# Re-planned RWKV and MLP-mixer kernel: new transfer costs, wide transposes of u, a row of w by matmul, and zero products in the head

## The chip, the cores and the metric

The kernel runs on one core of one Trainium2 chip. The metric is the device time of one execution in microseconds (us). A core has five engines with instruction streams of their own: TensorE (PE; its weight loads are listed as PEld), VectorE (DVE), ScalarE (ACT), GpSimd (POOL) and SyncE (SP), and 16 DMA engines that move data for all of them. Each stream runs in order; streams wait for one another through semaphores.

## The reference

A linear-attention recurrence with per-channel decay (RWKV) gives `x`, and a token-and-channel MLP mixer follows. B = 4 batches, H = 8 heads, S = 768 steps, D = 48 channels per head; `x` is 768 x 384 per batch.

```python
def _attn_ref(r, k, v, w, u):
    state = np.zeros((B, H, D, D))
    for t in range(S):
        kt, vt, rt = (k[:, :, t], v[:, :, t], r[:, :, t])
        cur = np.einsum('bhd,bhe->bhde', u[None] * kt, vt)
        y[:, :, t] = np.einsum('bhd,bhde->bhe', rt, state + cur)
        state = w[None, :, :, None] * state + np.einsum('bhd,bhe->bhde', kt, vt)
    return y

def _moe_ref(x, w_tok1, w_tok2, w_ch1, w_ch2):
    xt = x.transpose(0, 2, 1)
    h = np.maximum(xt @ w_tok1, 0.0) @ w_tok2       # 768 -> 256 -> 768, over tokens
    u = x + h.transpose(0, 2, 1)
    h2 = np.maximum(u @ w_ch1, 0.0) @ w_ch2         # 384 -> 1536 -> 384, over channels
    return u + h2
```

Note that the name `u` stands for two things: the bonus row `u` of the recurrence (8 x 48 numbers, an input beside the decay row `w`), and the mixer's middle value `u` (768 x 384 per batch, `u_sb` in the kernel, `uT` when turned).

## The kernel before, in words

**Tiling.** The recurrence is done in chunks of T = 128 steps: 24 *units*, six per batch (C = 6), numbered over all batches. Powers of the decay are folded into `k` and `r` with two tables per position in a group of G = 3 chunks: `wn` (for `k`) and `wp` (for `r`), made on ACT from `lnw = ln w`. For one unit:

- `load` brings k, r and v (192 KB each; tiles `ld_k`, `ld_r`, `ld_v`), issued by SP.
- `kp` and `rp` multiply k and r by their tables into `kpr` (POOL or DVE, as the plan chooses); `vb` casts v on ACT.
- k and r are turned: either on TensorE (`tr`, eight 128x128 transposes into PSUM, copied out by `rk` on ACT) or by one DMA transpose that SP issues (`turn_unit`). `CFG["turned"]` lists the units that use DMA.
- `at` is the 128x128 product of the turned k and r for every head, in two PSUM tiles of four heads; `AT` masks each into SBUF on DVE. In units of `CFG["raw"]` the second tile is first cast by ACT (`raw`) and then masked from SBUF (`ATr`).
- `pr`, `pg`, `adg` and `yd` give the bonus term, `kv` and `S` the state, `yS` and `y` the output of the chunk, and `x` adds `y` and `yd` into the batch's `x_b`.

**The mixer of a batch.** `hid` accumulates the token product into two PSUM tiles while units finish; `hr` is its relu; for each of the six chunks `bk` is the way back and `us` adds it to `x_b` (tile `u_sb`). Then `u` is turned: in batches of `pe_turn` on TensorE (`tu`, three transposes per chunk, copied out by `uT`), in the others by one DMA transpose per chunk (`uTd`). Each half of a batch (`sg`, three chunks) then has 12 `z` steps (three products each, relu by `zr`) and, for each chunk, 12 products `h`, with `os` and the store `out` behind them. The four weight matrices are fetched by POOL's DMA queue.

**The order.** No loop sets the order of the work. `graph` describes all steps with their engine, busy time and the time until a reader sees the result; `Plan.run` is a list scheduler over these numbers, which picks for every step an engine and a start. The kernel emits the steps in order of planned start, and each engine's order is kept as emitted. The plan's times are never used on the chip: only the order and the choice of engine come from them. Loads are held back by buffer space (eight units ahead); the loads of unit 6 also wait for `rp` of unit 5, so that the weights pass first. Tiles in PSUM beyond those of the recurrence share four buffers (pool `psM`, tag "m"); the plan keeps count of them in `banks`.

**The start.** `w` is broadcast to 128 partitions by a DMA of 192 KB on ACT's queue (`w_bc`); `w` and `u` are also loaded as eight rows each (`rows`) by SP after the first v, for a small product `wu`. TensorE runs eight products on a tile of zeros (`idle`) before the first real one.

Of the kernel before, what the change touches and what calls it, by code (L numbers as in the profile page):

```python
# [20 lines left out]
Ln = ACTF.Ln  # L21

B, H, S, D = 4, 8, 768, 48
T = 128
# [20 lines left out]
class Plan:  # L45
# [3 lines left out]
    def __init__(self, banks, busy_until, in_flight):  # L49
        self.steps, self.banks, self.busy_until, self.in_flight = [], banks, busy_until, in_flight  # L50

# [19 lines left out]
    def run(self):  # L71
# [5 lines left out]
        while todo:  # L77
# [4 lines left out]
            while again:  # L82
                again = False
                for s in sorted(open_, key=lambda s: (s.rank, s.ready)):
                    if s.ready > now or (s.take and min(banks) > now):
                        continue
                    if s.sends is not None and len(sent) >= self.in_flight:
                        old = sent[-self.in_flight]
                        if old.seen is None or old.seen > now:
                            if old.seen is not None:  # L90
                                heapq.heappush(times, old.seen)
                            continue
                    way = min(s.ways, key=lambda w: max(now, free.get(w[0], 0.0)) + w[2] + (w[4] if len(w) > 4 else 0.0))
                    eng, busy, seen = way[:3]
                    shares = len(way) > 3 and way[3]
                    if free.get(eng, 0.0) > now:
                        continue
                    if shares and port["DVE" if eng == "POOL" else "POOL"] > now:
                        heapq.heappush(times, max(port.values()))
                        continue  # L100
                    s.engine, s.start, s.end, s.seen = eng, now, now + busy, now + seen
                    free[eng] = s.end
                    if s.sends is not None:
                        sent.append(s.sends)
                    if shares:
                        port[eng] = s.end
                    heapq.heappush(times, s.end)
                    if s.take:
                        i = banks.index(min(banks))
                        banks[i], held[s.name] = float("inf"), i  # L110
                    for g in s.give:
                        banks[held.pop(g)] = s.seen
                        heapq.heappush(times, s.seen)
# [10 lines left out]
        return sorted(self.steps, key=lambda s: s.start)  # L124


MM = 0.1625
# [6 lines left out]
def graph(do, cfg):  # L134

    p = Plan(4, cfg.get("busy_until", dict(ACT=3.0, DVE=3.3, POOL=3.6)), cfg.get("in_flight", 8))
    unit_rank = cfg.get("unit_rank", lambda u: u)
# [7 lines left out]

    tables = {0: p.add("tables0", [("ACT", 1.6, 1.75)], rank=-100, emit=do("tables", 0))}
    setup = tables[0]
    for g in (1, 2):
        tables[g] = p.add(f"tables{g}", [("ACT", 1.05, 1.2)], [setup], rank=g - 0.6, emit=do("tables", g))

    wu = p.add("wu", [("PE", 0.6, 0.8)], rank=0.05, emit=do("wu"))
    uw = p.add("uw", [("DVE", 0.65, 0.8)], [wu], rank=0.05, emit=do("uw"))
# [4 lines left out]
    for n, (kind, i) in enumerate(cfg["transfers"]):  # L157
        if kind == "u":
            for nm in cfg.get("lorder", "krv"):
                s = p.add(f"i:{nm}{i}", [("SP", 0.45, 0.6)], fetched[-1:], rank=-1000 + n, emit=do("load", nm, i))  # L160
                fetched.append(s)
                gates[nm, i] = s
                loads[nm, i] = p.transfer(f"x:{nm}{i}", s, 0.93, 1.9, 0.0)
        else:
# [3 lines left out]
    def weight(i, after):  # L168
        s = p.add(f"i:w{i}", [("POOL", 0.9, 1.0, True)], after, rank=-50, emit=do("weight", i))
        took = cfg.get("wtime", (3.3, 3.0, 7.0, 7.8))[i]  # L170
        wx[i] = p.transfer(f"x:w{i}", s, took, took + 1.0, -1.0)

    p.wait(wu, [loads["v", 0]])
    wafter = cfg["wafter"]
    xs, S_prev, at_free, y_free, kv_read, yS_prev = {}, None, [], None, None, None
    kv_first, bank_read = None, []
    for u in range(NU):
# [9 lines left out]
        kp = p.add(f"kp{u}", [POOL2, DK], [loads["k", u], tab, old], rank=r, emit=do("kp", u))  # L187
        rp = p.add(f"rp{u}", [POOL2, DK], [loads["r", u], tab, old], rank=r + 0.1, emit=do("rp", u))
        for i, after in wafter.items():
# [51 lines left out]
    for b in range(B):  # L241
# [8 lines left out]
        hr = [p.add(f"hr{b}_{i}", [ACT1, DVEP], [h], give=[f"hid{b}_bank{i}"], rank=r, emit=do("hr", b, i)) for i in range(2)]  # L250
        uT = []
        for c in range(C):
# [5 lines left out]
            else:  # L258
                s = p.add(f"i:uT{b}_{c}", [("SP", 1.25, 1.3)], [us], rank=-3000 + c, emit=do("uTd", b, c))
                uT.append(p.transfer(f"x:uT{b}_{c}", s, 0.4, 1.3, 0.0))  # L260
        for sg in range(2):
# [7 lines left out]
            for si in range(3):  # L269
# [4 lines left out]
                downs[-1].append(s)  # L274
                s = p.add(f"i:o{b}_{c}", [("SP", 0.35, 0.4)], [s], rank=-1500, emit=do("out", b, c))
                stores.append(p.transfer(f"x:o{b}_{c}", s, 0.6, 1.8, 0.0))
    rng = random.Random(cfg.get("seed", 0))
# [19 lines left out]
def kernel(  # L297
# [53 lines left out]
    act.preload_act_table_set("natural_log_exp_and_others")  # L351


    idle = const.tile([128, 512], bf16, name="idle")
    dve.memset(idle, 0.0)
    idle_ps = psM.tile([128, 512], f32, name="idle_ps", tag="m")
    for _ in range(CFG.get("warm", 0)):
        pe.matmul(idle_ps, idle[:, 0:128], idle, start=True, stop=True)


    rows = const.tile([2 * HP, 2, P], f32, name="rows")
    dve.memset(rows, 1.0)
    iota_i = const.tile([128, 2, G], i32, name="iota_i")
# [42 lines left out]

    def tables(eng, g):
        if g == 0:
            act.activation(lnw, w_bc, Ln)
        act.activation(wn[:, g, :], lnw, Exp, scale=iota[:, 1, g:g + 1])  # L410
        act.activation(wp[:, g, :], lnw, Exp, scale=iota[:, 0, g:g + 1])

# [5 lines left out]
    def uw(eng):  # L418
        dve.tensor_copy(wu_sb, M0["wu"])
        for q in range(2):  # L420
            half = slice(q * P, q * P + P)
            dve.tensor_mul(UW[half, :, q], wu_sb[half, 0, :], wu_sb[half, 1, :])

    wtok1 = wts.tile([128, 6, dtok], bf16, name="wtok1")
# [10 lines left out]
    def load(eng, nm, i):  # L435
# [8 lines left out]
        loaded[nm, i] = t  # L444
        if (nm, i) == ("v", 0):
            for j, src in enumerate((w, u)):
                sp.dma_start(rows[j * HP:j * HP + HP, :, 0:D], src.rearrange("(a q) d -> a q d", q=2))
            if wide:
                sp.dma_start(out=u_bc, in_=u.rearrange("h d -> (h d)")[None, :].to_broadcast([128, dm]))

# [145 lines left out]
    def hid(eng, b, c):  # L596
        if c == 0:
            M[b]["h1"] = [psM.tile([128, dm], f32, name="h1_ps", tag="m") for _ in range(2)]
            M[b]["h1r"] = mpool.tile([128, 2, dm], bf16, name="h1r")
            M[b]["u"] = mpool.tile([128, C, dm], bf16, name="u_sb")  # L600
            M[b]["uT"] = mpool.tile([128, 3, S], bf16, name="uT")
        for i in range(2):
# [24 lines left out]
    def uT(eng, b, c):  # L627
        to = M[b]["uT"][:, :, ts(c, 128)]
        if eng == "ACT":
# [3 lines left out]

    def uTd(eng, b, c):
        sp.dma_start_transpose(M[b]["uT"][:, :, ts(c, 128)], M[b]["u"][:, c, :])

    def z(eng, b, sg, j):
# [3 lines left out]
        for m in range(3):  # L641
            pe.matmul(M[b]["z", sg, j], wch1[:, m, ts(j, 128)], M[b]["uT"][:, m, ds(sg * 384, 384)],
                      start=(m == 0), stop=(m == 2))
# [15 lines left out]
    def out_(eng, b, c):  # L659
        sp.dma_start(out[b, ts(c, 128), :], M[b]["o", c])  # L660

    STEPS = {
        "tables": tables, "wu": wu, "uw": uw, "load": load, "weight": weight, "gd": gd, "wGm": wgm, "kp": kp, "rp": rp,
        "vb": vb, "ku": ku, "rku": rku, "adg": adg, "yd": yd, "turn_unit": turn_unit,
# [8 lines left out]

    for s in graph(do, CFG).run():
        if s.emit is not None:
# [31 lines left out]
```

## Time and profile before

Three runs: 187.84, 188.04 and 188.58 us, median 188.04. The profiled execution took 188.54 us; its span, from the first to the last instruction, is 186.8 us.

| engine | busy us | share of the span | instructions |
|---|---|---|---|
| PE | 160.3 | 86% | 1440 |
| PEld | 99.1 | 53% | 1440 |
| DVE | 97.1 | 52% | 199 |
| ACT | 85.5 | 46% | 183 |
| POOL | 61.9 | 33% | 77 |

How to read it: a row of a timeline has the start, the length (both us), the engine, the operation, output<-input, and how many instructions were merged; in square brackets stands the idle time before it and what ended it. SPq is the sync engine's queue of DMA issues: its length is the time to issue, not to move the data. A row of the waits has who waited for whom, the sum of us, how often, and the longest. A group row has shapes, count, busy us, mean ns, and the idle time before. Matmuls are pipelined and overlap in their records. The granted clock is TensorE's, as a share of full speed. The DMA share is that of the 16 DMA engines, and can print above 1 where transfers overlap.

### The profile page before, as it was taken

How to read it: one execution, taken by the hardware profiler on the slowest of the kernel's cores; microseconds unless marked ns; L12 is line 12 of the kernel's file. 1: busy time of each engine (PE TensorE's matmuls, PEld its weight loads, DVE VectorE, ACT ScalarE, POOL GpSimd, SP SyncE). 2: the span in 40 equal slices, each digit the busy share in tenths (PEclk: the TensorE clock that was granted, in tenths of full speed). 3: DMA queues.
4: the chain of work that ended last, by engine and by line, in shares of the span. 5: the costliest groups of instructions: out<-in, count | busy, mean ns of one | idle time of the engine just before them, and what ended most of it. 6: DMA issues, size and time to landing. Idle time of an engine off the chain costs nothing.

```text
span 186.8 us, 3768 instructions
## 1 busy us (share of the span) xinstructions
PE 160.3 (86%) x1440; PEld 99.1 (53%) x1440; DVE 97.1 (52%) x199; ACT 85.5 (46%) x183; POOL 61.9 (33%) x77
## 2 busy tenths in 40 slices
PE   7458778799999999658979899974999999999992
PEld 2346555365666666434546454542656566556650
DVE  3279965650289877951834678734526702102121
ACT  2868555189538642017332473120551290652800
POOL 4208700044087699330185456511501000000000
PEclk9999999999999999979999999998799999999999
DMA  4899999999769899946899999749631352302103
GB/s 96 161 219 215 190 204 200 186 201 214 149 165 197 170 216 159 204 80 125 181 190 208 208 204 241 130 82 210 159 58 42 63 67 91 120 0 88 42 2 126
DMA packets 101690, 27.38 MB, mean 147 GB/s; under 512 B 95528, under 2 KB 101288, under 8 KB 101672
## 3 DMA queue, kind: packets, MB, share of 16 engines
q1 hardware_dynamic: 98520, 23.80, 62.6%
q0 software_dynamic: 3008, 3.15, 10.2%
q10 hardware_dynamic: 144, 0.20, 0.5%
q8 instruction: 11, 0.18, 0.4%
q14 instruction: 7, 0.06, 0.1%
HBM read 20.65 MB, written 4.72 MB: 136 GB/s over the span
## 4 chain that ended last, share of the span: by engine, by line
PE 53%; DVE 13%; DMA 12%; SPq 6%; issue 6%; ACT 4%; POOL 4%; POOLq 0%; DVEq 0%; ACTq 0%
PE h_ps L338 21%; PE z_ps L338 21%; SPq L338 6%; DMA ld_k<-in_k_dram 4%; DVE AT L338 3%; DMA ld_r<-in_r_dram 3%; PE hT_ps L338 3%; PE y_ps L338 3%; POOL kpr L338 2%; DMA ld_v<-in_v_dram 2%; DVE x_b L338 2%; DVE u_sb L338 2%; ACT rk L338 2%; PE at_ps L338 2%; PE tr_ps L338 2%
## 5 line engine op out<-in xcount | busy, mean ns | idle before, releaser
L338 ACT ACTIVATE zr<-z_ps 128x384 bf16<-128x384 f32 x95 | 46.2, 491 | 35.8 <-PE z_ps L338 35.7
L338 PE MATMUL z_ps<-uT,wch 128*128 128x384 bf16 x288 | 56.4, 337 | 1.6 <-DMA uT<-u_sb 1.6
L338 PE MATMUL h_ps<-wch,zr 128*128 128x384 bf16 x288 | 55.2, 326 | 0.0
L338 PEld LDWEIGHTS <-wch 128*128 128x128 bf16 x288 | 27.6, 100 | 19.4 <-issue 4.2
L338 PEld LDWEIGHTS <-zr 128*128 128x128 bf16 x288 | 26.6, 97 | 15.6
L338 POOL TENSOR_TENSOR yd<-vb,adg 128x384 f32<-128x384 bf16 x19 | 15.7, 828 | 45.3 <-ACT adg L338 44.9
L338 DVE TENSOR_TENSOR osb<-u_sb,h_ps 128x384 f32<-128x384 bf16 x24 | 13.0, 550 | 33.8 <-PE h_ps L338 33.7
L338 POOL TENSOR_TENSOR kpr<-ld_k,wn 128x384 bf16<-128x384 f32 x21 | 21.3, 1015 | 24.0 <-DMA ld_k<-in_k_dram 18.7
L338 DVE TENSOR_TENSOR AT<-at_ps,mask 128x512 bf16<-128x512 f32 x42 | 27.6, 683 | 2.1 <-PE at_ps L338 1.9
L338 POOL TENSOR_TENSOR kpr<-ld_r,wp 128x384 bf16<-128x384 f32 x20 | 20.6, 1028 | 9.1 <-DMA ld_r<-in_r_dram 5.7
L338 DVE TENSOR_TENSOR pr<-rk 128x512 bf16<-128x512 bf16 x24 | 12.2, 512 | 15.0 <-DMA rk<-kpr 11.3
L338 DVE TENSOR_TENSOR x_b<-y_ps,yd 128x384 bf16<-128x384 f32 x24 | 13.3, 553 | 11.8 <-PE y_ps L338 6.8
L338 PEld LDWEIGHTS <-kpr 128*128 128x128 bf16 x176 | 13.5, 113 | 9.7 <-DVE kpr L338 3.4
L338 PEld LDWEIGHTS <-rk 48*128 48x128 bf16 (+1 forms) x272 | 11.1, 101 | 14.0 <-DMA rk<-kpr 6.4
L338 ACT CAST vb<-ld_v 128x384 bf16<-128x384 f32 x24 | 12.2, 510 | 12.7 <-DMA ld_v<-in_v_dram 12.7
L338 ACT COPY rk<-tr_ps 128x1024 bf16<-128x1024 bf16 x12 | 12.1, 1010 | 9.6 <-PE tr_ps L338 7.6
L338 PE MATMUL at_ps<-rk 48*128 48x128 bf16 x192 | 10.6, 237 | 5.2 <-DMA rk<-kpr 4.1
L338 PE MATMUL tr_ps<-ident,kpr 128*128 128x128 bf16 x96 | 11.9, 265 | 2.7 <-DVE kpr L338 2.3
L338 DVE TENSOR_TENSOR S<-kv_ps,bm 128x384 bf16<-128x384 f32 x13 | 7.2, 553 | 13.1 <-PE kv_ps L338 10.6
L338 PE MATMUL h_ps<-x_b,wtok 128*128 128x384 bf16 x48 | 12.4, 348 | 1.5 <-DVE x_b L338 1.5
L338 DVE TENSOR_TENSOR u_sb<-x_b,hT_ps 128x384 bf16<-128x384 bf16 x24 | 11.9, 550 | 1.5 <-PE hT_ps L338 1.5
L338 PEld LDWEIGHTS <-wtok 128*128 128x128 bf16 x96 | 8.8, 100 | 6.9 <-issue 2.6
(58 smaller groups left out, 109.1 us busy)
## 6 DMA issues: line engine op xcount, KB each, us to landing
ld_k<-in_k_dram SPq DMA_DIRECT2D x24, 192.0 KB, 3.6
ld_r<-in_r_dram SPq DMA_DIRECT2D x24, 192.0 KB, 4.0
ld_v<-in_v_dram SPq DMA_DIRECT2D x24, 192.0 KB, 3.7
out_dram<-osb SPq DMA_DIRECT2D x24, 192.0 KB, 2.0
wch<-in_moe_w_ch_dram POOLq DMA_DIRECT2D x2, 1152.0 KB, 14.4
wtok<-in_moe_w_tok_dram POOLq DMA_DIRECT2D x2, 384.0 KB, 6.6
uT<-u_sb SPq DMA_TRANSPOSE x18, 2.4
w_bc<-in_w_dram ACTq DMA_DIRECT2D x1, 192.0 KB, 3.9
```

Source lines behind the costliest of these rows:

```text
L338: return lambda *args, **kw: tc.keep_in_program_order(f(*args, **kw))
```

## The change

1. The plan's costs: a load is 0.60 us of SP and 1.01 of DMA (0.45 and 0.93 before), a turn by DMA 1.35 and 1.56 (1.25 and 1.0), a store 0.57 and 0.63, the weights 3.0, 2.6, 6.2 and 7.7 us; the engines' first free times change, and the tables become separate steps (`lnw`, `wn`, `wp`), so that `rp` waits for `wp` alone.
2. The mixer's `u`: in batches 0 and 1 it is turned on TensorE; in batches 2 and 3 by two DMA transposes of three chunks each. The tile `uT` is laid out by chunk, so that `z` reads three pieces of 128 columns.
3. The row of `w` is fetched once (1.5 KB) and spread over 128 partitions by a product with a column of ones; `lnw` reads it from PSUM. The `rows` loads move from SP to ACT's queue at the start.
4. TensorE runs two products on zeros before that product and ten behind it (eight in all before). Up to the first `z`, each planned pause of TensorE of at least 0.3 us gets products on zeros (256 columns) that by the plan last until 0.15 us before its end.
5. Units 12 and 13 are turned on TensorE, `raw` is dropped, and the first two weight loads come one unit later in the plan.

```diff
+    def fill(self, until, least, margin, each, emit):
+        mine = sorted((s for s in self.steps if s.engine == "PE"), key=lambda s: s.start)
+        for a, b in zip(mine, mine[1:]):
+            if b.start > until:
+                break
+            taken = sum(1 for x in self.used if x[0] < b.start and x[1] > a.end)
+            n = int((b.start - a.end - margin) / each)
+            if b.start - a.end >= least and taken < self.banks and n > 0:
+                s = self.add(f"fill{a.name}", [("PE", n * each, n * each)], emit=emit(n))
+                s.engine, s.start, s.end, s.seen = "PE", a.end, a.end + n * each, a.end + n * each
...
-            s = p.add(f"i:t{u}", [("SP", 1.25, 1.3)], [kp, rp], rank=-2000, emit=do("turn_unit", u))
-            rk = p.transfer(f"x:t{u}", s, 1.0, 2.2, 0.0)
+            s = p.add(f"i:t{u}", [("SP", 1.35, 1.4)], [kp, rp], rank=-2000, emit=do("turn_unit", u))
+            rk = p.transfer(f"x:t{u}", s, 1.56, 2.2, 0.0)
...
-                s = p.add(f"i:uT{b}_{c}", [("SP", 1.25, 1.3)], [us], rank=-3000 + c, emit=do("uTd", b, c))
-                uT.append(p.transfer(f"x:uT{b}_{c}", s, 0.4, 1.3, 0.0))
+                some.append(us)
+                if c % G == G - 1:
+                    s = p.add(f"i:uT{b}_{c}", [("SP", 1.35, 1.4)], some, rank=-3000 + c, emit=do("uTd", b, c // G))
+                    uT += [p.transfer(f"x:uT{b}_{c}", s, 1.75, 2.4, 0.0)] * G
+                    some = []
...
-    wafter={0: 3, 1: 4, 2: 5, 3: 5},
+    wafter={0: 4, 1: 5, 2: 5, 3: 5},
     hold={6: ("rp", 5)},
-    turned=range(12, 24),
-    raw=range(6),
+    turned=range(14, 24),
+    pe_turn=(0, 1),
     kr0=0.2, yd0=0.1,
     cold=1.0,
-    warm=8,
+    fill=(0.3, 0.15, 0.107),
...
-    w_bc = const.tile([128, dm], f32, name="w_bc")
-    act.dma_start(out=w_bc, in_=w.rearrange("h d -> (h d)")[None, :].to_broadcast([128, dm]))
+    row = const.tile([1, 2, dm], f32, name="row")
+    rows = const.tile([2 * HP, 2, P], f32, name="rows")
+    dve.memset(rows, 1.0)
...
+        if j == 0 or wide:
+            act.dma_start(out=row[:, j, :], in_=src.rearrange("h d -> (h d)")[None, :])
+    for j, src in enumerate((w, u)):
+        act.dma_start(rows[j * HP:j * HP + HP, :, 0:D], src.rearrange("(a q) d -> a q d", q=2))
...
+    warm(CFG.get("warm", (2, 10))[0])
+    pe.matmul(w_ps, ones, row[:, 0, :], start=True, stop=True)
+    warm(CFG.get("warm", (2, 10))[1])
...
-    def uTd(eng, b, c):
-        sp.dma_start_transpose(M[b]["uT"][:, :, ts(c, 128)], M[b]["u"][:, c, :])
+    def uTd(eng, b, sg):
+        half = slice(sg * G, sg * G + G)
+        sp.dma_start_transpose(M[b]["uT"][:, half].rearrange("p c m t -> p (c m) t"),
+                               M[b]["u"][:, half].rearrange("p c n -> p (c n)"))
...
+    def fill(eng, n):
+        t = psM.tile([128, 256], f32, name="fill_ps", tag="m")
+        for _ in range(n):
+            pe.matmul(t, idle[:, 0:128], idle[:, 0:256], start=True, stop=True)
...
+    plan = graph(do, CFG)
+    steps = plan.run()
+    if CFG.get("fill"):
+        first = next(s for s in steps if s.name == "z0_0_0").start
+        steps = plan.fill(first, *CFG["fill"], lambda n: lambda eng: fill(eng, n))
+    for s in steps:
```

More of the change, by code (lines that the diff above doesn't have):

```diff
@@ L110, in run @@
                         banks[i], held[s.name] = float("inf"), i
+                        self.used.append([now, float("inf"), s.name])
                     for g in s.give:
                         banks[held.pop(g)] = s.seen
+                        next(x for x in self.used if x[2] == g)[1] = s.seen
                         heapq.heappush(times, s.seen)
@@ L134, in graph @@
 def graph(do, cfg):
-    p = Plan(4, cfg.get("busy_until", dict(ACT=3.0, DVE=3.3, POOL=3.6)), cfg.get("in_flight", 8))
+    p = Plan(4, cfg.get("busy_until", dict(ACT=3.85, DVE=3.6, POOL=3.6, PE=5.0)), cfg.get("in_flight", 8))
     unit_rank = cfg.get("unit_rank", lambda u: u)
@@ L356, with warm @@
     idle_ps = psM.tile([128, 512], f32, name="idle_ps", tag="m")
[L357 to L362, printed above, removed]
+    w_ps = psM.tile([128, dm], f32, name="w_ps", tag="m")
+    def warm(n):
+        for _ in range(n):
+            pe.matmul(idle_ps, idle[:, 0:128], idle, start=True, stop=True)
+    warm(CFG.get("warm", (2, 10))[0])
+    pe.matmul(w_ps, ones, row[:, 0, :], start=True, stop=True)
+    warm(CFG.get("warm", (2, 10))[1])
+    if wide:
+        u_ps = psM.tile([128, dm], f32, name="u_ps", tag="m")
+        pe.matmul(u_ps, ones, row[:, 1, :], start=True, stop=True)
     iota_i = const.tile([128, 2, G], i32, name="iota_i")
@@ L444, in load @@
         loaded[nm, i] = t
[L445 to L449, printed above, removed]
     def weight(eng, i):
@@ L672, in do @@
         return lambda eng: STEPS[kind](eng, *args)
-    for s in graph(do, CFG).run():
+    def fill(eng, n):
+        t = psM.tile([128, 256], f32, name="fill_ps", tag="m")
+        for _ in range(n):
+            pe.matmul(t, idle[:, 0:128], idle[:, 0:256], start=True, stop=True)
[5 more added lines that the diff above has]
+    for s in steps:
         if s.emit is not None:
```

49 lines of the change are left out of this document (29 added, 20 removed).

## The prediction

> **What bounds the kernel now.** I read the per-stretch table first, then TensorE's waits, then the sync engine's queue (SPq) in order of time, then single instructions. Rows of the per-stretch table: stretch, length, busy time (instructions) of PE, PEld, DVE, ACT and POOL, granted clock, DMA share, GB/s.
>
> ```profile
> 8.00:38.57 30.57, 23.17 (x246) 15.83 (x247) 23.41 (x47) 17.69 (x39) 8.59 (x9) 1.00 1.16 202
> 38.57:183.10 144.53, 133.08 (x1187) 81.76 (x1184) 70.74 (x138) 63.81 (x139) 50.08 (x54) 0.98 0.67 138
> 40.00:130.00 90.00, 78.64 (x814) 49.03 (x812) 54.31 (x106) 39.19 (x87) 44.93 (x49) 0.98 0.89 176
> 76.70:82.34 5.64, 2.15 (x37) 1.42 (x37) 4.93 (x10) 0.33 (x2) 2.61 (x3) 0.93 0.66 138
> 82.34:85.76 3.42, 3.42 (x21) 1.89 (x22) 0.56 (x1) 1.31 (x3) 0.00 (x0) 0.62 0.44 86
> 124.90:128.62 3.72, 0.28 (x3) 0.01 (x2) 0.03 (x1) 0.32 (x1) 0.00 (x0) 1.00 0.71 134
> 129.37:132.80 3.43, 3.43 (x25) 1.85 (x24) 2.11 (x5) 1.45 (x4) 1.45 (x2) 0.51 1.07 249
> 35.00:40.00 5.00, 4.46 (x38) 2.82 (x37) 3.92 (x8) 2.69 (x7) 0.99 (x1) 1.00 1.27 196
> ```
>
> There are two regimes. From the first `z` product at 38.57 to the last product at 183.10 TensorE is the bound: busy 133.08 of 144.53 us, so 11.45 us idle. All but 0.1 of that idle lies between 40 and 130 (78.64 of 90). Two holes hold most of it, 76.70 to 82.34 (3.49 idle) and 124.90 to 128.62 (3.44 idle), and behind each stands a stretch of 3.4 us at a granted clock near 0.5 to 0.6. Before 38.57 no engine is full, and DMA is (share 1.16 from 8 us on).
>
> ```profile
> PE at_ps L338 <- DMA rk<-kpr: 4.1, 2, 3.4
> PE kv_ps L338 <- ACT vb L338: 1.6, 1, 1.6
> PE z_ps L338 <- DMA uT<-u_sb: 1.6, 1, 1.6
> ```
>
> TensorE's longest waits end with DMA transposes. The sync engine's queue shows why:
>
> ```profile
> 70.57 3.06 SPq L338 DMA_TRANSPOSE rk<-kpr  x1
> 75.18 1.37 SPq L338 DMA_TRANSPOSE rk<-kpr  x1
> 77.27 7.71 SPq L338 DMA_TRANSPOSE uT<-u_sb  x6
> 90.49 2.76 SPq L338 DMA_DIRECT2D ld_r<-in_r_dram  x1
> 116.91 8.33 SPq L338 DMA_TRANSPOSE uT<-u_sb  x6
> 125.34 2.63 SPq L338 DMA_TRANSPOSE rk<-kpr  x2
> 145.05 8.20 SPq L338 DMA_TRANSPOSE uT<-u_sb  x6
> ```
>
> Six transposes of `u` hold this in-order queue for about 8 us per batch. The turns of the recurrence (`rk`) and all loads stand behind them: `rk` issued at 125.34 is what TensorE waits for until 128.62. In batch 1 the first three `uT` are what `z` waits for until 82.34. In batch 3 (145.05) TensorE has other products throughout, so those 8.2 us cost nothing now.
>
> **The change, part by part.** The sum is made against the profiled execution: span 186.8 us, time 188.54 us, so 1.74 us lie around the span. The three timed runs have their median at 188.04, 0.5 below it.
>
> *Wide transposes.* What does one cost?
>
> ```profile
> L338 SPq DMA_TRANSPOSE uT<-u_sb x18: 1185/1206/1773, 77.3 to 152.0; - x18
> DMA to landing us min/median/max: 2.3/2.4/4.1
> L338 SPq DMA_TRANSPOSE rk<-kpr x12: 1231/1436/3056, 70.6 to 135.4; - x12
> DMA to landing us min/median/max: 3.1/3.5/5.1
> ```
>
> `uT` moves 384 columns, `rk` 1024: 2.7 times the size takes 1.44 instead of 1.21 us to issue and 3.5 instead of 2.4 to land. The new one has 1152 columns, nearest to `rk`: about 1.5 us of the queue and 3.7 us to land. Two per batch hold the queue 3.0 us where six held 8. (Bounds: 1.2, if only the number of issues counts, to 3.6, if columns do.) `z` of half a batch then needs one landing of its own half.
>
> *Batch 2 (term H).* The `rk` issue at 125.34 moves up by 8.33 - 3.0 = 5.3 us to about 120, lands near 123.5, and TensorE runs out of other work only at 125.2. The hole of 3.44 goes, and with it the slow stretch behind it:
>
> ```profile
> 39.88 6.99 PE L338 MATMUL z_ps<-uT,wch 128*128 128x384 bf16 x42
> 82.34 2.08 PE L338 MATMUL z_ps<-uT,wch 128*128 128x384 bf16 x6 [1.56 <-DMA uT<-u_sb]
> 129.37 3.08 PE L338 MATMUL z_ps<-uT,wch 128*128 128x384 bf16 x9
> ```
>
> Forty-two `z` products in 6.99 us are one per 0.163; nine in 3.08 are one per 0.32. So the stretch at 129.37 costs 9 x 0.157 = 1.4 us, and that at 82.34 (six `z`, then some small products) about 1.3. H = -3.4 - 1.4, with 0.5 left for what is late next (the loads behind it): **-4.3** (bounds -2.5 and -4.8).
>
> *Batch 1 (E, F).* Its `u` is now turned on TensorE, as in batch 0, so the six issues leave the queue and `z` waits for no DMA: E = -3.5 idle - 1.3 slow = **-4.8**. Units 12 and 13 are also turned on TensorE (the two issues at 70.57 and 75.18 go).
>
> ```profile
> 39.23 0.17 PE t_ps L338 x3
> 48.82 0.22 PE tr_ps L338 x4
> ```
>
> TensorE gains 6 x 0.17 + 4 x 0.22 = 1.9, say 2.0 us, wholly on the bound. The copies out of PSUM (six of `uT`, two of `rk`) fall to ACT and DVE; ACT is busy 0.33 of the 5.64 us there, which hides them. Without that cover I would double the term, hence its upper bound. In batch 0 this mixing step left TensorE 0.54 us idle from 35 to 40; I take 0.5 for batch 1. F = **+2.5** (2.0 to 5).
>
> *Loads (G).* With twelve microseconds gone from the queue between 70 and 85, the loads issued at 88 to 91 go out earlier. TensorE waited 1.6 for `vb` and 0.7 of the 4.1 for `rk` in that region: 2.3 in all. Since the DMA share is already 0.89 over 40 to 130, I count two thirds: **-1.5** (0 to -2.3).
>
> *Head.* The rows:
>
> ```profile
> 1.27 3.60 PE L338 MATMUL idle_ps<-idle 128*128 128x512 bf16 x8 [1.27 <-DVE idle L338]
> 4.65 0.83 SPq L338 DMA_DIRECT2D rows<-in_w_dram  x1
> 5.52 0.63 SPq L338 DMA_DIRECT2D rows<-in_u_dram  x1
> 8.00 4.22 DMA ld_k<-in_k_dram
> 20.33 0.48 PE y_ps L338 x4
> 29.60 0.44 PE tr_ps L338 x4
> 27.17 0.61 PE L338 MATMUL at_ps<-rk 48*128 48x128 bf16 x8 [0.68 <-ACT rk L338]
> 31.13 0.40 PE L338 MATMUL at_ps<-rk 48*128 48x128 bf16 x8 [0.23 <-ACT rk L338]
> ```
>
> A: both `rows` loads leave the sync queue, which is on the chain until the load at 8.00: **-1.5** (0.83 + 0.63; bounds 0, where DMA is full anyhow, and -2.4, if the 192 KB broadcast that goes counts too). The Trainium skill ("DMA: Bandwidth & Descriptors", section "Issuing engines are not separate DMA queues") says that a second issuing engine saves only the time on the sequencer; by it A ends at 1.5.
>
> B: the head runs on the slow clock, though the table prints 1.00 there: eight `at` take 0.61 at 27.17 and 0.40 at 31.13. The chain from 20.33 to 29.60 has nine TensorE pieces, which sum to 4.4 us. At 0.40/0.61 they take 2.9, so **-1.5** if the zero products keep the clock up (bounds 0 and -3, the second if all waits that follow shrink too). The eight warm products of 3.60 us did not raise it; twelve and the `w` row product are longer, and zeros now fill the pauses. The Trainium skill ("TensorE: Matmul & The Clock Gate", section "Part 4: PE-mode transpose") says that the full clock does not engage for transposes; by it three of the nine pieces would stay slow and B would be -1.0. The trace differs: four `tr` take 0.22 at 48.82 against 0.44 at 29.60.
>
> C: `raw` goes; the second half of `AT` comes straight out of PSUM on DVE.
>
> ```profile
> L338 DVE TENSOR_TENSOR AT<-at_ps,mask 128x512 bf16<-128x512 f32 x42 | 27.6, 683 | 2.1 <-PE at_ps L338 1.9
> L338 ACT CAST raw<-at_ps 128x512 bf16<-128x512 f32 x6 | 3.5, 587 | 1.3 <-PE at_ps L338 1.2
> L338 DVE TENSOR_TENSOR AT<-raw,mask_b 128x512 bf16<-128x512 bf16 x6 | 2.5, 424 | 0.2 <-ACT raw L338 0.2
> ```
>
> DVE pays 6 x 0.26 = 1.6 more, ACT 3.5 less. DVE is on the chain about half the head: **+0.8** (-0.6, one `raw` off the chain, to +1.6).
>
> D: zeros stand in TensorE's program order, and each group takes one of the four shared PSUM buffers. A pause that comes out shorter than planned, or a buffer whose reader is late, delays the product queued behind the zeros and the DVE step that waits for it. Each group is planned 0.15 us short of its pause: **+0.5** (0 to 3.4, one stretch as long as the slow one at 82.34).
>
> Taken at nothing: the first weight load goes one unit later.
>
> ```profile
> 17.01 1.00 POOL L338 DMA_DIRECT2D wtok<-in_moe_w_tok_dram  x1
> 28.02 0.84 PE L338 MATMUL h_ps<-x_b,wtok 128*128 128x384 bf16 x2
> ```
>
> It has 11 us from issue to first use; a unit of the head takes some 4 (estimate: six units between 8 and 34), so 7 are left; if that were not enough, it would cost what it is late. The strided read of `uT` in `z`: no row shows it; a tenth more on 288 `z` at 0.163 would be 4.7 us, and nothing says that a product could gain. The corrected costs also reorder every step after the first few. No row prices that; the idle behind the first `z` bounds it, and I leave 3 us either way for it in the range.
>
> **Sum:** head -1.5 - 1.5 + 0.8 + 0.5 = -1.7; middle -4.8 + 2.5 - 1.5 - 4.3 = -8.1; together -9.8. 188.54 - 9.8 = **178.7 us**.
>
> **Rivals.** *Everything pays.* TensorE is left with hardly a pause and the head takes its better bounds: -6 in the head would be extreme; -4 there and -9.5 in the middle give about 175. For it: the middle is pure TensorE work once DMA is early. Against: small waits are spread over all stretches.
>
> *DMA becomes the bound.* Over 40 to 130 DMA works 0.89 x 90 = 80 us. My middle needs the share to go to about 0.98. If it stops at 0.93, 80 us of transfers take 86, so the middle gains 4: 188.54 - 1.7 - 4 = about 183. For it: the head at 1.16 shows DMA full. Against: the same figure shows that a share near 1 can be held, and two turns and six small transposes leave the engines.
>
> *Slower: zeros on a cold clock.* Place: TensorE's in-order stream from 8 to 38.57. It is busy 23.2 us there on the slow clock; on the fast one 23.2 x 0.66 = 15.3, so a plan made for the fast clock sees some 15 us of pauses and fills perhaps 10 (an estimate). If the clock stays down, these take 20, the head's stream is 43 instead of 31 us, and the time 188.5 + 12.6 - 8.1 = 193. It decides where zeros cost over 8.1 us more than they bring. For it: 3.6 us of warm products left the clock down. Against: it rose at about 31 behind a run of dense products, so a dense stream raises it itself.
>
> *The zeros do nothing:* the clock stays down and the pauses are real. B is 0, D about 0.5: 180.2 to 181.
>
> **How the numbers follow.** Forecast 0.57; everything pays 0.12; zeros do nothing 0.09; DMA bound 0.12; cold zeros 0.10. The unknown costs move the forecast by about 4 either way (174.5 to 183); the better ends of B and G below 175, and the worse ends of C, D and G above 183, stretch that to 173.5 and 186, which leaves out most of the cold zeros and little else. A measurement of this kernel tells about 0.5% from no change. Faster by more than that needs under 187.1: 0.86. Slower 0.10, from cold zeros; within 0.5% 0.04, a DMA bound with a late head.
>
> **What would show it.** Right: two issues of `uT` each for batches 2 and 3, near 1.5 us apiece; no TensorE hole over 1 us near 77 to 82 or 125 to 128; granted clock near 1 from 40 us on; TensorE idle of about 5 us behind the first `z`; eight `at` in about 0.40 before 25 us; first `z` at 36 to 38. Wrong: `at` still at 0.61 with zeros between; the wide transpose over 2.5 us of queue; TensorE idle over 9 us again behind the first `z`; `z` above 0.17 per product in dense runs.

## The result and the profile after

The kernel after takes 175.01 us (median of four runs, 174.71 to 175.59), the kernel before 188.31 beside it: a ratio of 0.9296 (95% interval 0.9256 to 0.9336), 13.3 us faster. The forecast was 178.7 us with a range of 173.5 to 186.0. The profiled execution took 175.59 us, its span is 173.9.

The kernel before took 188.3 to 191.4 us beside the several runs below, so runs of different groups are compared by their ratio to it. Two of the four executions each with narrow transposes (179.30 and 179.72 us) and with the old figures (179.88 and 180.25) were in a slower state and are left out of their times. A ratio difference of 0.01 is 1.9 us.

The per-stretch table of after, from its first `z` to its last product, and a stretch of the head (columns as before):

```profile
37.00:170.13 133.13, 131.07 (x1219) 82.15 (x1219) 72.71 (x138) 67.00 (x144) 49.72 (x54) 1.00 0.73 147
20.00:22.00 2.00, 1.78 (x34) 1.43 (x35) 2.00 (x5) 1.30 (x6) 1.98 (x3) 1.00 0.00 0
```

The products now take 133.13 us where they took 144.53, with 2.06 us idle in place of 11.45. The first `z` moved from 38.57 to 37.00. So 11.4 us come from the middle (from the first `z` to the last product) and 1.6 from the head (what stands before). All of TensorE's waits from 36 us on:

```profile
PE z_ps L358 <- DMA wch<-in_moe_w_ch_dram: 1.7, 1, 1.7
PE kv_ps L358 <- DVE S L358: 1.1, 1, 1.1
PE kv_ps L358 <- DVE pr L358: 0.7, 2, 0.5
```

No wait for `rk`, `uT` or `vb` is left. The first row is new: the first `z` waits for the channel weights. In the stretch of the head above, from 20 to 22 us, no transfer runs (DMA share 0.00). The clock row of the page (granted clock in 40 slices), before and then after:

```profile
PEclk9999999999999999979999999998799999999999
```

```profile
PEclk9999999999999999999999999999999999999999
```

The two dips behind the two holes are gone. For the head this row can't be used: it prints 9 before, too, where eight `at` took 0.61. In the run "batch 1 on TensorE alone" below, which has the same head as before, the granted clock is printed as 0.51 from 8 to 20 us, with `at` at 0.61 as well. The sync engine's transposes of `u`, in order of time, and then the view of the tile `uT` with their lengths in ns and the time to landing:

```profile
107.04 2.73 SPq L358 DMA_TRANSPOSE uT<-u_sb  x2
134.71 1.28 SPq L358 DMA_TRANSPOSE uT<-u_sb  x1
136.73 1.31 SPq L358 DMA_TRANSPOSE uT<-u_sb  x1
```

```profile
L358 SPq DMA_TRANSPOSE uT<-u_sb x4: 1285/1308/1332, 107.0 to 136.7; - x4
DMA to landing us min/median/max: 3.2/3.2/3.5
```

A batch holds the queue for 2.6 to 2.7 us where it held it for 8.

### The profile page after: what moved, and what is told of

It reads as the page before. It is cut to its first block, busy times and chain, and to the rows that moved or that the text cites. A ratio compares the mean times of both kernels' runs of the same rounds, so it can differ in the third digit from the quotient of the medians.

```text
span 173.9 us, 3938 instructions
## 1 busy us (share of the span) xinstructions
PE 161.9 (93%) x1543; PEld 101.0 (58%) x1543; DVE 100.0 (58%) x201; ACT 84.6 (49%) x179; POOL 63.8 (37%) x80
## 4 chain that ended last, share of the span: by engine, by line
PE 70%; DVE 10%; DMA 8%; ACT 4%; issue 3%; POOL 2%; DVEq 0%; ACTq 0%
PE h_ps L358 28%; PE z_ps L358 23%; DMA wch<-in_moe_w_ch_dram 8%; ACT zr L358 3%; PE kv_ps L358 3%; PE y_ps L358 3%; PE at_ps L358 3%; PE idle_ps L358 3%; DVE AT L358 3%; PE tr_ps L358 2%; PE hT_ps L358 2%; DVE pr L358 2%; DVE S L358 1%; DVE u_sb L358 1%; POOL kpr L358 1%
## 5 line engine op out<-in xcount | busy, mean ns | idle before, releaser
L358 PE MATMUL z_ps<-uT,wch 128*128 128x384 bf16 x288 | 52.9, 326 | 1.7 <-DMA wch<-in_moe_w_ch_dram 1.7
L358 DVE TENSOR_TENSOR AT<-at_ps,mask 128x512 bf16<-128x512 f32 x48 | 31.2, 683 | 10.6 <-PE at_ps L358 10.4
L358 POOL TENSOR_TENSOR yd<-vb,adg 128x384 f32<-128x384 bf16 x21 | 17.6, 837 | 41.5 <-ACT adg L358 36.1
L358 POOL TENSOR_TENSOR kpr<-ld_k,wn 128x384 bf16<-128x384 f32 x20 | 20.1, 1007 | 15.6 <-DMA ld_k<-in_k_dram 15.6
L358 POOL TENSOR_TENSOR kpr<-ld_r,wp 128x384 bf16<-128x384 f32 x22 | 21.9, 997 | 8.0 <-DMA ld_r<-in_r_dram 4.4
L358 ACT COPY rk<-tr_ps 128x1024 bf16<-128x1024 bf16 x14 | 14.2, 1012 | 9.6 <-PE tr_ps L358 9.5
L358 ACT COPY adg<-kv_ps 128x8 f32<-128x8 f32 x21 | 3.5, 166 | 26.5 <-PE kv_ps L358 26.0
L358 DVE TENSOR_TENSOR x_b<-y_ps,yd 128x384 bf16<-128x384 f32 x24 | 13.3, 554 | 5.2 <-PE y_ps L358 4.6
L358 PEld LDWEIGHTS <-kpr 128*128 128x128 bf16 x192 | 12.3, 97 | 4.3 <-DVE kpr L358 0.9
L358 DVE TENSOR_TENSOR pr<-rk 128x512 bf16<-128x512 bf16 x24 | 14.8, 618 | 0.0
L358 PE MATMUL h_ps<-x_b,wtok 128*128 128x384 bf16 x48 | 11.4, 326 | 0.0
L358 PEld LDWEIGHTS <-AT 128*128 128x128 bf16 x192 | 8.2, 96 | 4.4 <-DVE AT L358 2.3
```

The source lines that it names most:

```text
L358: return lambda *args, **kw: tc.keep_in_program_order(f(*args, **kw))
```

## The experiments

**Without zeros.** After, with `fill=(0.3, 0.15, 0.107)` removed from `CFG`; the warm products at the start stay.

> The changed kernel without the zero products in the pauses of the head; the emitted order is otherwise the same, and the products on zeros at the very start stay. Clock theory (the prediction's term B, 1.5 us): without zeros the clock falls back before 20 us, eight at take 0.61 again, the first z comes 1 to 3 us later than 37.0, and the time is 176 to 178. Weights theory: the first z waits for the landing of the channel weights (13.7 us from issue, in the trace of the changed kernel), so with the same weight issue times TensorE may be up to 2 us later for nothing: time 174.5 to 175.5, although at is slow. If the start's products alone keep the clock up: at stays at 0.40 and the time is 174.5 to 175.2.

Measured: 176.15 us, ratio 0.9322 (0.9228 to 0.9415). Three rows of the per-stretch table, and from the timeline two `at`, a later wait and the first `z`:

```profile
11.80:15.20 3.40, 2.10 (x36) 1.51 (x37) 3.40 (x6) 1.91 (x5) 1.78 (x2) 0.97 1.03 204
15.00:22.20 7.20, 6.34 (x83) 5.24 (x84) 6.89 (x13) 3.27 (x8) 5.61 (x7) 0.53 0.68 131
32.00:36.00 4.00, 3.46 (x18) 1.92 (x17) 2.77 (x5) 0.88 (x3) 0.92 (x1) 0.57 1.11 196
```

```profile
13.62 0.40 PE L357 MATMUL at_ps<-rk 48*128 48x128 bf16 x8
15.00 0.27 PE L357 MATMUL kv_ps<-UW,pr 128*128 128x2 bf16 x4 [0.70 <-DVE pr L357]
17.47 0.61 PE L357 MATMUL at_ps<-rk 48*128 48x128 bf16 x8 [0.35 <-ACT rk L357]
38.05 0.66 PE L357 MATMUL z_ps<-uT,wch 128*128 128x384 bf16 x3 [0.95 <-DMA wch<-in_moe_w_ch_dram]
```

The longer warm-up alone has the clock up at 13.62 (`at` in 0.40 us), but it falls twice, to 0.53 and 0.57. In the kernel after, whose emitted order is otherwise the same, all six groups of eight `at` in the head take 0.40: there the zeros hold the clock, as the clock theory had it. What that is worth is less clear. The first `z` comes at 38.05 without zeros; the kernel after had 37.00, and the two runs with zeros on this same chip, below, 37.19 and 36.83. But it waits for the channel weights in all of these, for 0.95, 1.66, 1.97 and 0.64 us. TensorE was done with what comes before at 37.10 without zeros, and at 35.34, 35.22 and 36.19 with them, so 0.9 to 1.9 us earlier. These are single executions, and with zeros, too, a first `z` at 38.20 is seen further down. The whole time shows 0.0026 of the ratio, or 0.5 us, which lies inside the intervals.

**Narrow transposes.** After, with six transposes of 384 columns again in batches 2 and 3.

```diff
-        sp.dma_start_transpose(M[b]["uT"][:, half].rearrange("p c m t -> p (c m) t"),
-                               M[b]["u"][:, half].rearrange("p c n -> p (c n)"))
+        sp.dma_start_transpose(M[b]["uT"][:, c], M[b]["u"][:, c, :])
```

> The changed kernel with six transposes of u per batch in batches 2 and 3 as before (with their old plan costs), instead of two wide ones. Queue theory (the prediction's term H): the six hold the sync queue for about 8 us in batch 2, turns and loads wait behind them, TensorE gets a hole of 2 to 4 us near 110 to 120 with a slow stretch behind it: 177.5 to 180. Cover theory: TensorE now has the z and h of batch 1 left at that time (they started earlier), which cover the queue: 175 to 176.

Measured: 176.33 and 177.23 us, ratio 0.9361 (0.9253 to 0.9469). The sync engine's queue, and TensorE's first `z` and longest wait of batch 2, in the execution that took 179.30 us:

```profile
106.85 9.69 SPq L355 DMA_TRANSPOSE uT<-u_sb  x6
116.65 4.03 SPq L355 DMA_TRANSPOSE rk<-kpr  x3
```

```profile
37.19 0.66 PE L355 MATMUL z_ps<-uT,wch 128*128 128x384 bf16 x3 [1.97 <-DMA wch<-in_moe_w_ch_dram]
119.93 0.40 PE L355 MATMUL at_ps<-rk 48*128 48x128 bf16 x8 [1.55 <-DMA rk<-kpr]
```

In this trace the hole is back, at 1.55 us rather than two to four, and no slow stretch follows it (granted clock 1.00 from 119 to 124). But the execution was 2 to 3 us longer than the two above, and its clock also fell to 0.61 from 37 to 41, long before the first transpose of `u` by DMA at 106.85. Whether the shorter executions had the hole is not shown. By the ratios the wide form is worth about 1.2 us with the rest of the change in place, but their intervals overlap. So neither theory is settled here; the two times lie between their ranges.

**Batch 1 by wide transposes.** After, with `pe_turn=(0,)` in place of `(0, 1)`.

> The changed kernel with batch 1's u turned by two wide DMA transposes instead of on TensorE (18 products and six copies fewer). Landing theory (terms E, F): z of batch 1 waits for the landing of the first half, about 3.5 us behind the third u_sb, with little other work left for TensorE there: a hole of 1.5 to 3 us near 76 to 80, less 1.0 us of TensorE work: 175.5 to 178. Work theory: TensorE's work alone counts, so the 1 us less of it shows: 173.8 to 174.5.

Measured: 177.15 us, ratio 0.941 (0.9302 to 0.9518), about 2 us above after, though the intervals overlap. TensorE has 18 transposes less to do, and yet the products take 134.87 us in place of 133.13:

```profile
36.83:171.70 134.87, 130.51 (x1201) 81.47 (x1201) 72.11 (x139) 64.80 (x137) 49.72 (x54) 1.00 0.75 151
```

```profile
PE kv_ps L358 <- DVE S L358: 2.3, 3, 1.1
```

Busy time falls by 0.56 and idle time rises from 2.06 to 4.36. The time is as the landing theory had it, but its wait is not there: no row has TensorE waiting for `uT`. The second row shows TensorE's longest wait behind the first `z`, which ends with the state `S` of the recurrence. From 74 to 84 us TensorE is idle for 1.46 us, against 0.21 in the kernel after, and the pause before the first `z` of batch 1 (0.91 us, until 81.80) is one for `S`. TensorE lacks the work that would cover it. The emitted order changes from 67 us of the plan on, and whether the later `uT` or the order left that gap is open.

**The old plan figures.** After, with the load, weight, turn and store costs of before.

```diff
-[("SP", 0.6, 0.65)]  ... 1.01, 2.1      # load; likewise turn and store
+[("SP", 0.45, 0.6)]  ... 0.93, 1.9
-(3.0, 2.6, 6.2, 7.7)
+(3.3, 3.0, 7.0, 7.8)
```

> The kernel after, with the plan's transfer and issue figures of the kernel before put back (loads 0.45/0.93, weights 3.3, 3.0, 7.0 and 7.8, turn issue 1.25 with 1.0, store 0.35/0.6); everything else, wide transposes, matmul rows of w, zeros, stays. The emission order alone can change by it. Theory 1 (the corrected figures do no work of their own; the gain is that of the instructions): within 0.6 us of the kernel after beside it. Theory 2 (the corrected figures move loads and products into better places; they carry the 3.3 us of the middle that the forecast lacked): 1.5 to 3.5 us above the kernel after, with holes of TensorE over 0.5 us behind loads or rk between 60 and 130 us.

Measured: 177.04 and 177.08 us, where the kernel before had a median of 191.37; the quotient, 0.925, for which there is no interval, is no worse than the 0.9296 of the kernel after. Its products' stretch and its longest wait:

```profile
37.77:171.64 133.87, 130.58 (x1216) 82.29 (x1213) 70.35 (x139) 67.17 (x143) 48.24 (x53) 1.00 0.72 146
```

```profile
PE at_ps L358 <- DMA rk<-kpr: 1.8, 2, 1.1
```

The products take 0.74 us more than after, with 1.8 us of waits for `rk`, one of them 1.1 us long, which is a sign that theory 2 named; the first `z` came at 37.77. But the traces are of different chips, and the quotient shows no loss. So theory 1 fits better: the corrected figures do not carry the 3.3 us of theory 2, and that they carry anything is not shown.

**Wide transposes alone.** Before, with the wide transposes, their plan costs and the new layout of `uT`.

> The kernel before, with one part of the change: u turned by two transposes of 1152 columns in place of six of 384 in each batch, and the layout of uT for it. Theory 1 (SP's queue sets rk's time; the six issues took 6.85 to 9.7 us of it): the hole of the third batch (3.44 us with the slow stretch of 1.4 us behind it) goes, and part of that of the second (uT itself lands earlier or later by under 1 us): 3.0 to 5.5 us below the kernel before, so 183 to 185.5 where that shows 188.5. Theory 2 (a transfer, not the issue, is late: the wide transpose lands as late as the six): within 1 us of the kernel before, and the hole is still there under another name.

**Batch 1 on TensorE alone.** Before, with `pe_turn=(0, 1)`.

> The kernel before, with one part of the change: u of the second batch turned by TensorE, too. Theory 1 (the sum of the forecast): hole of 3.5 us and slow stretch of 1.3 us go, transposes add about 2.1 us of TensorE: 2 to 3.5 us below the kernel before, 185 to 186.5. Theory 2 (the issues that this frees on SP's queue bring the later rk and loads forward too, so that a share of the third batch's hole goes with them): 4 to 6 us below, 182.5 to 184.5.

Measured: 182.56 us, ratio 0.9574 (0.9505 to 0.9643), and 185.31 us, 0.9717 (0.9644 to 0.979). The products' stretch and TensorE's longest wait, wide transposes alone first:

```profile
39.73:177.24 137.51, 132.30 (x1186) 82.73 (x1184) 72.34 (x141) 62.86 (x136) 50.17 (x54) 0.98 0.73 148
```

```profile
PE z_ps L341 <- ACT zr L341: 1.5, 2, 1.3
PE at_ps L341 <- DMA rk<-kpr: 0.2, 1, 0.2
```

```profile
36.96:178.92 141.96, 131.56 (x1205) 82.59 (x1202) 72.28 (x143) 64.97 (x140) 50.52 (x54) 0.99 0.73 144
```

```profile
PE at_ps L339 <- DMA rk<-kpr: 5.9, 4, 3.6
```

By these windows the first takes 7.0 us out of the middle and the second 2.6, against a trace of the kernel before that was taken where it ran in 188.54 us and not in 191.37. By the ratios, which count the head as well, it is 8.2 and 5.4 us. After the second, the hole behind `rk` stands where it stood, 3.6 us; after the first, no wait for a transfer above 0.2 us is left (its rows above are the longest wait and the one for `rk`). So the first bears out theory 1, with more gain than its 3.0 to 5.5 us. For the second the ratio lies in theory 2's range and the windows in theory 1's, but theory 2's reason is not there, since the hole of the third batch stayed.

What the second did with the idle time is not what theory 1 had. The hole of batch 1 is gone, but other waits came (for `rk` 1.24 and 0.67 us near 100, for `adg` 1.70 at 85, for `pr` 1.79 at 115): TensorE is idle for 10.40 us in place of 11.45, and its busy time falls by 1.52. In the first, idle time falls from 11.45 to 5.21; of batch 1's hole 2.6 us stay, which are waits for VectorE (79 to 83). Both edits also change the emitted order, from 67 us of the plan on.

The two heads show how far single traces can be trusted there. By the plan both runs have the order of the kernel before up to 67 us, and yet the first `z` came at 39.73 and 36.96, where the kernel before had 38.57. The first also lays out `uT` otherwise, but its head was behind already at the products on the way back (`hT_ps`, 35.58 against 33.83). So a first `z` can differ by 2.8 us between executions of one order on one chip.

**`raw` kept.** After, with `raw=range(6)`.

> The kernel after, with the raw form of the first six units kept as in the kernel before (the scaling left to the later operation), which the change dropped. Theory 1 (the forecast's term of +0.8 us for dropping it): 0.5 to 1.0 us below the kernel after, with the first z 0.5 to 1 us earlier. Theory 2 (the first z waits for the channel weights, issued late on GpSimd's queue, so nothing that VectorE saves in the head shows): within 0.4 us of the kernel after, the first z at 36.5 to 37.5 still behind the weights.

Measured: 187.41 us, ratio 0.9847 (0.977 to 0.9924). Neither theory had that. A piece of the chain, and the timelines of VectorE and TensorE:

```profile
29.10 11.10 DMA ld_k<-in_k_dram
```

```profile
28.52 0.55 DVE L359 TENSOR_TENSOR kpr<-ld_r,wp 128x384 bf16<-128x384 f32 x1
```

```profile
26.00 0.61 PE L359 MATMUL at_ps<-rk 48*128 48x128 bf16 x8
41.41 0.61 PE L359 MATMUL tr_ps<-ident,kpr 128*128 128x128 bf16 x4 [8.61 <-POOL kpr L359]
50.38 1.79 PE L359 MATMUL z_ps<-uT,wch 128*128 128x384 bf16 x10
```

In this plan k of unit 6 passes the DMA queue ahead of the second weight, at 24.1 us, so its transpose is ordered before the last products of the first batch. On the chip `rp` of unit 5, for which this load is held, ran on VectorE at 28.52 and not at 22.8 as planned; the load went out at 29.10, behind all weights, and arrived at 40.2. TensorE, in order, stood 8.61 us before that transpose. The run says nothing of `raw`; it prices a wrong order. It also shows zeros that did not hold the clock: behind a pause of 1.64 us (21.63 to 23.26) eight `at` took 0.61 at 26.00.

**Weights earlier in the plan.** After, with `wafter={0: 3, 1: 4, 2: 5, 3: 5}`; and the same **without zeros**.

> The changed kernel with the first two weight loads one unit earlier in the plan (as in the kernel before). Weights theory: the DMA engines stand still from about 19 to 22.5 us in the changed kernel because the weights are issued late; filling that hole brings the landing of the channel weights and the first z (37.0) forward by 1.5 to 2 us: 173 to 173.7. Head theory: TensorE and DVE set the first z anyway, or the loads of units 4 and 5 are slowed as much by the weights beside them: 174.6 to 175.5.

> The kernel with the weights due earlier in the plan, which took 188.2 us, with the zeros left out. Theory 1 (the 118 zero products in a pause that only the plan has are what costs): back to 175 to 178 us, first z at 37 to 39. Theory 2 (the order is at fault: the plan's one queue for transfers puts the transposes of units 6 and 7 ahead of the first batch's last products, and TensorE, which works in order, meets them there while their loads land behind the weights): first z still at 48 to 51, 183 to 185.5 us; the zeros were only the part above that, 3 to 5 us.

Measured: 188.18 us, ratio 0.9938 (0.9894 to 0.9983); without zeros 184.24 us, 0.9689 (0.962 to 0.9758). From TensorE's timeline, with zeros and then without, and between them the cast of unit 5's v with zeros:

```profile
32.93 13.04 PE L358 MATMUL fill_ps<-idle 128*128 128x256 bf16 x118
54.13 0.65 PE L358 MATMUL z_ps<-uT,wch 128*128 128x384 bf16 x3
```

```profile
30.88 0.52 ACT L358 CAST vb<-ld_v 128x384 bf16<-128x384 f32 x1
```

```profile
41.56 0.61 PE L357 MATMUL tr_ps<-ident,kpr 128*128 128x128 bf16 x4 [4.11 <-POOL kpr L357]
49.20 0.65 PE L357 MATMUL z_ps<-uT,wch 128*128 128x384 bf16 x3
```

The plan has one queue for transfers and put v of unit 5 behind all weights, at 39.4; on the chip its cast began at 30.88. Neither theory of the first run held: both had 173 to 175.5 us. The 118 zeros were laid into a pause that did not exist. But without them the first `z` still comes at 49.20: again the transposes of unit 6 are ordered too early. Against after (0.9296) the order, without any zeros, costs 0.039 of the ratio, 7.4 us (8.6 us against after again, below, on the same chip), and the zeros another 0.025, 4.7 us by the ratios of two chips. The order theory of the last expectation holds.

**Weights sent earlier on GpSimd.** After, with the planned order kept but for two lines.

```diff
     steps = plan.run()
+    at = {s.name: s for s in steps}
+    at["i:w0"].start = at["yd2"].start - 0.01
+    at["i:w1"].start = at["rp4"].start + 0.01
+    steps.sort(key=lambda s: s.start)
```

> The kernel after, once more, as the yardstick on the chip of the three runs beside it: 0.926 to 0.934 of the kernel before, first z at 37.0.

> The kernel after with its plan and order on all engines kept, but for two lines of GpSimd's: the first weight's issue goes ahead of yd of unit 2 (in the 0.87 us for which GpSimd waited there), the second's behind rp of unit 4. Theory 1 (the first z waits 1.66 us for channel weights that were issued late, while the DMA engines stood idle from 20 to 22 us; nothing else is late there): first z at 35.2 to 35.8, all later work as before, 1.2 to 1.8 us below the kernel after. Theory 2 (VectorE and the turned chunks are late by nearly as much, or the loads of units 6 to 8 end last): first z 36.5 to 37, within 0.4 us of the kernel after. Theory 3 (the weights now collide with the loads of unit 5): first z later than 37.2 and 0.3 us or more above.

Measured on one chip: after again 175.65 us, ratio 0.9246 (0.9202 to 0.9289); weights sent earlier 174.16 us, 0.9156 (0.9118 to 0.9193). The first `z`, after again and then with the weights sent earlier, and in the latter the first weight's issue:

```profile
38.20 0.66 PE L358 MATMUL z_ps<-uT,wch 128*128 128x384 bf16 x3 [2.02 <-DMA wch<-in_moe_w_ch_dram]
```

```profile
35.98 0.65 PE L358 MATMUL z_ps<-uT,wch 128*128 128x384 bf16 x3
18.53 1.01 POOL L358 DMA_DIRECT2D wtok<-in_moe_w_tok_dram  x1
```

The wait for the weights is gone and the time falls by 1.5 us, with intervals that do not overlap: theory 1. This version beats both kernels. After again, the ratio came out just below its expected range, and the first `z` 1.2 us later than in the first profile of the same kernel. Since a first `z` differs by that much and more between executions, a gain of a microsecond in the head is read from the times of several executions, not from two traces.

**Weights earlier, `raw` kept.** The last version with `raw=range(6)`, and the load of unit 6 placed behind the weights in the plan.

> The run with the weights sent earlier, and the raw copies of the first six units kept on ScalarE, with the load of unit 6 placed behind the weights in the plan, so that the transposes of unit 6 stay behind the first batch's products. Theory 1 (the forecast's term: 0.26 us of VectorE for each of six units, half of it on the way to the first z): first z 0.5 to 1.0 us earlier than without the copies, 0.5 to 1.0 us below it. Theory 2 (VectorE has slack in the head by then): within 0.4 us. Theory 3 (ScalarE's copy lies on the way itself, and the order gets worse): first z 0.5 us or more later and as much above.

Measured: 177.23 us, ratio 0.9301 (0.9252 to 0.9349), 3.1 us above the version it is built on. Its first `z`, and VectorE's groups that answer to it:

```profile
39.12 7.96 PE L360 MATMUL z_ps<-uT,wch 128*128 128x384 bf16 x48
```

```profile
L360 DVE TENSOR_TENSOR AT<-raw,mask_b 128x512 bf16<-128x512 bf16 x6 | 3.1, 522 | 0.0
L360 DVE TENSOR_TENSOR yd<-vb,adg 128x384 f32<-128x384 bf16 x5 | 3.5, 710 | 0.0
```

Theory 3: the first `z` is 3.1 us later. VectorE saves 6 x 0.16 us in the masks (0.68 without the copy), but the planner now gives it five `yd` of 0.71 where it had three of 0.55, and nothing of the saving arrives. The clock fell, too: eight `at` took 0.61 at 21.98, behind a pause of 0.97 us (until 18.93). Copy, order and clock were not separated.

## Why the prediction was right

The sign and the range held, and so did the main mechanism, the queue of transposes. How the gain splits into the terms did not hold, and where sums agree some of it is luck. The forecast was 3.7 us too slow: 3.3 of it lie in the middle, and the rest is mostly that the profiled execution stands 0.6 above the median.

**Head: -1.7 predicted, -1.57 measured.** The agreement is partly luck, in two ways. First, these are two single traces, and a first `z` moved by up to 2.8 us between executions of one order. Second, TensorE was ready for `z` at 35.34, 3.2 us earlier than before, and the wait for the channel weights took 1.66 of that back. So by this trace the head without that wait gained more than the sum of A to D, and a term that the prediction took at nothing cost the rest: the first weight one unit later. "7 us are left" counted to the token product; the matrices queued behind it, which `z` needs, had no slack. Sending the first two weights earlier gave 1.5 us of time.

The single terms are not measured apart. Of B and D, -1.0 together, the run without zeros leaves out the zeros in the pauses but keeps the longer start; they had TensorE ready 0.9 to 1.9 us earlier. The rule of the Trainium skill that was weighed there ("TensorE: Matmul & The Clock Gate", section "Part 4: PE-mode transpose") would have made B + D -0.5. The traces differ from it: four `tr` took 0.63 us in the slow stretch of the run without zeros (at 15.73) and 0.39 in the kernel after (at 15.27). For A, SP's load of unit 2 goes out 2.74 us earlier (5.26 for 8.00):

```profile
5.26 0.75 SPq L358 DMA_DIRECT2D ld_k<-in_k_dram  x1
```

How much of that reached the first `z` is open. C's +0.8 was never seen: keeping `raw` made the head later in both runs, in the first through the plan's order, in the second with order and clock changed beside it.

**Middle: -8.1 predicted, -11.4 measured.** The cause, the sync engine's queue, is shown by the two runs that each do one part alone: wide transposes take the waits for `uT` and `rk` away, and with six narrow ones left in the third batch its hole stays, at 3.6 us. E + F was -2.3 and batch 1 on TensorE alone gives -2.6, but this, too, agrees by luck. E and F had 3.0 us less idle time and 0.7 more busy time; the run has 1.05 and 1.52 less, and it leaves out units 12 and 13. H was -4.3 for batch 2; wide transposes alone give -7.0, since they shorten batch 1's block as well, which the prediction left to E. The gains overlap: with everything else in place the wide form, now in two batches only, is worth about 1.2 us by the ratios, whose intervals overlap.

Which term takes the missing 3.3 us, by the windows: 2.0 are idle time (2.06 where the terms left 4.0; G and the residues in H and F were sized for stalls that hardly came) and 1.3 are busy time (131.07 where -2.7 + 2.0 left 132.4). About 0.5 of the 1.3 is F's price of a transpose: the 18 of batch 1 were put at 1.0 us, and leaving them out lowered TensorE's busy time by 0.56. The rest is open. The wide issue of 1.31 us was close to the 1.2 at which only the number of issues counts; the prediction took 1.5. The corrected figures, for which it left 3 us either way, moved the middle by 0.74 between two chips' traces.

**The rivals.** Everything pays, at about 175, is where the time came out, though by the middle rather than the head. DMA did not become the bound: its share over the products went to 0.73 from 0.67 and TensorE waited for it only at the first `z`. The zeros did something: without them the clock fell. The slower rival did not happen, but zeros that cost more than they bring exist: those that wait out a pause of the plan cost 4.7 us in the run with early weights, on a clock that was up (118 of them in 13.04 us are one per 0.11). There the condition was a wrong pause, not a cold clock.

**The signs.** Two issues per batch of 1.3 us, no hole over 1 us near 77 to 82 or 125 to 128 (the longest behind the first `z` is 1.10 us, until 65.32), clock at 1.00, first `z` at 37.00: as named. `at` before 25 us:

```profile
11.39 0.40 PE L358 MATMUL at_ps<-rk 48*128 48x128 bf16 x8
```

TensorE's idle time was to be about 5 us and is 2.06: the one sign that missed.

## What to carry to other kernels

Where one in-order queue feeds several late readers, price what empties it once for the queue, not once per hole: here the wide transposes alone took 7.0 us out of the middle where the forecast gave them one hole of 4.3, and with the other remedy beside them they were worth less, about 1.2 us by the ratios. When a sum agrees, compare its parts as well: twice here two misses cancelled. When a head gets faster, look for the issue that was put late because nothing waited for it; here two lines gave 1.5 us more. In a kernel ordered by a plan, a small edit can put one in-order product ahead of a load that is late on the chip; it cost some 7 and 10 us in two runs, more than any cost it was meant to change.

## What the runs showed of the hardware

- A DMA transpose of 1152 columns took 1.31 us to issue and 3.2 to land, one of 384 took 1.21 and 2.4 (medians in the kernels after and before): three times the columns for 8% more of the queue.
- Without zeros the granted clock fell from 1.00 to 0.50 at about 15 us, behind a stretch (11.80 to 15.20) in which TensorE was busy 2.10 of 3.40 us and had no pause above 0.70 us. The Trainium skill ("TensorE: Matmul & The Clock Gate", section "Why this matters for your kernels") asks for no idle gaps above about 3 us between bursts; here the clock fell behind shorter ones.
- Products on zeros in those gaps kept eight `at` at 0.40 us throughout the head of the kernel after. They did not in three runs with another order: eight `at` took 0.61 with `raw` kept (at 26.00), with the weights earlier in the plan (at 23.09) and in the last run (at 21.98). Pauses of 1.64, 2.40 and 0.97 us that no zeros filled stood ahead of them.
